# Decode step on one core: batch rows eight times each, one output transfer that closes the program, and another last part of wd

## The chip, the cores and the metric

One core of a Trainium2 chip. The metric is the device time of one execution in microseconds (us). Beside it the profile gives a *span*, from the first to the last recorded instruction; the time is always larger, by 1.6 to 2.0 us here. (The record does not say where the time begins; below, all of the difference is put at the end of the span.) Engines: PE (matmul; PEld is its weight load), DVE (vector), ACT (scalar), POOL (GpSimd), SP (sync, which issues most transfers).

## The reference

Batch 4, one query token, model width D = 640, 32 heads of 192, 4096 cached positions, MLP width F = 1536, all bf16:

```python
x  = A_x                                            # (4, 1, 640)
h  = x + attention(layernorm(x), k_cache, v_cache, wq) @ wo
h2 = h + (silu(ln(h) @ w_gate) * (ln(h) @ w_up)) @ w_down   # ln = layernorm
return h2                                           # (4, 1, 640)
```

The two caches are (4, 32, 4096, 192), 201 MB each. Nearly all of the 424 MB that the kernel reads is cache.

## The kernel before

SP queues all bulk loads in order: wq, then the K and V tiles of 32 units (6.3 MB each), then wo, w_gate, w_up and w_down (`wd`). A unit is multiplied on DVE, summed on PE, exponentiated on ACT and multiplied with V on PE. The parts that the change touches are the dense layers around that loop. Each of those spreads over four 32-column groups of the PE: group n computes the n-th quarter of the output columns for the 4 batch rows, and puts them at partitions 32n to 32n+3.

```python
for lo, hi in ((0, 6), (6, 10), (10, CF)):          # wd in three transfers; CF = 12
    ...dma("sp", wdsb[:, lo:hi, :] <- wd rows lo:hi)
...
kot = op("dve", tensor_copy(OT[:, :, :] <- psT[:, 0:B * JW]))     # 192 elements per partition
for j in range(JW): womm(j)                         # 4 matmuls each, lhsT=OT[:, :, j]: 4 columns
zg = op("dve", memset(PB[0][:, 0:FQ], 0.0)); zg = op("dve", memset(PB[1][:, 0:FQ], 0.0))
ln2 = layer_norm(psH[:, 0:DQ], [wo_done])
...                                                 # gate and up: lhsT=lnT[:, c, 0:B]
for c in range(CF):
    for n in range(4):
        a = op("pe", matmul(psH[32 * n:32 * n + B, 0:DQ], lhsT=guT[:, c, 0:B],
                            rhs=wdsb[:, c, n * DQ:(n + 1) * DQ], ...), [gut, wd_land[c], ln2])
a = op("dve", tensor_copy(out=outsb[:, 0:DQ], in_=psH[:, 0:DQ]), [a])
fin = [dma("sp" if n < 2 else "act", out[:, 0, n * DQ:(n + 1) * DQ] <-
           outsb[32 * n:32 * n + B, 0:DQ], S_out, [a]) for n in range(4)]
with nc.Block() as block:
    pr.emit(block, [fin[-1]])                       # SP waits for all four; then the end barrier
```

## Time and profile before

| | before |
|---|---|
| time, median of the first 3 runs | 990.11 us (989.95 to 990.49) |
| span of the profiled run, its time | 988.26 us, 989.84 us |
| DMA | 429 GB/s mean over the span |
| busy: PE, DVE, ACT | 59%, 56%, 12% |

From the profile page of the kernel before: the mean busy share of the 16 DMA engines in 40 equal slices of the span (9 is 90% or more), and the packets of ACT's queue, q10.

```profile
DMA  9999999999999999999999999999999999999997
...
q10 hardware_dynamic: 48, 0.01, 0.0%
```

The transfers never stop until the last slice. So what gets faster *inside* that stream should be hidden by it. The chain that ended last shows where the stream lets go (start, us, what):

```profile
946.95 38.09 DMA wd_sb<-in_B_w_down_dram
985.03 0.04 issue
985.08 0.46 PE pb L571 x8
985.54 0.03 issue
985.57 0.32 DVE gu L574
```

What follows the wd load is exposed: eight matmuls, the DVE copy, the output and the end of the program. The timeline of the kernel before (start, us, engine, line, operation; in brackets the idle time before, and what ended it):

```profile
960.47 0.36 DVE L551 CAST OT<-pb 128x192 bf16<-128x192 f32 x1 [1.25 <-PE pb L497]
...
966.67 5.92 PE L504 MATMUL pb<-wo_sb,OT 128*4 128x160 bf16 x192 [6.23 <-DMA wo_sb<-in_A_wo_dram]
...
984.32 1.19 PE L571 MATMUL pb<-wd_sb,guT 128*4 128x160 bf16 x24 [0.48 <-DMA wd_sb<-in_B_w_down_dram]
985.08 0.10 PEld L571 LDWEIGHTS pb<-wd_sb,guT 128*4 128x4 bf16 x8 [0.39 <-DMA wd_sb<-in_B_w_down_dram]
985.57 0.32 DVE L574 CAST gu<-pb 128x160 bf16<-128x160 f32 x1 [2.76 <-PE pb L571]
985.92 0.67 SPq L575 DMA_DIRECT2D out_dram<-gu  x2
985.92 0.81 ACTq L575 DMA_DIRECT2D out_dram<-gu  x2
```

wd rows 6 to 9 are taken up at 984.32, rows 10 and 11 at 985.08: the PE waits for each. The wo and OT lines start long before, and wait for data. The end of the program in the view of its closing line (engine, operation, minimum/median/maximum in ns, first and last start); the branch is the first instruction after SP's wait for the output:

```profile
L578 POOLq DRAIN  x1: 611/611/611, 4.9 to 4.9; - x1
...
L578 SPq COMPARE_BRANCH  x1: 33/33/33, 987.7 to 987.7; - x1
...
L578 PEldq EVENT_SEMAPHORE  x1: 51/51/51, 988.0 to 988.0; - x1
...
L578 SPq EVENT_SEMAPHORE  x1: 17/17/17, 988.2 to 988.2; - x1
```

SP passes the last barrier about 0.2 us after the other engines.

### The profile page before, as it was taken

How to read it: one execution, taken by the hardware profiler on the slowest of the kernel's cores; microseconds unless marked ns; L12 is line 12 of the kernel's file. 1: busy time of each engine (PE TensorE's matmuls, PEld its weight loads, DVE VectorE, ACT ScalarE, POOL GpSimd, SP SyncE). 2: the span in 40 equal slices, each digit the busy share in tenths (PEclk: the TensorE clock that was granted, in tenths of full speed). 3: DMA queues.
4: the chain of work that ended last, by engine and by line, in shares of the span. 5: the costliest groups of instructions: out<-in, count | busy, mean ns of one | idle time of the engine just before them, and what ended most of it. 6: DMA issues, size and time to landing. Idle time of an engine off the chain costs nothing.

```text
span 988.3 us, 9469 instructions
## 1 busy us (share of the span) xinstructions
PE 579.3 (59%) x4409; PEld 129.0 (13%) x2941; DVE 553.3 (56%) x454; ACT 117.1 (12%) x376; POOL 3.7 (0%) x18
## 2 busy tenths in 40 slices
PE   1677555666555576556566655656665555765554
PEld 0011011110101111001111110111101011110023
DVE  2486555566645556655556665555666455566621
ACT  0311111110111110011111011111101111100120
POOL 1000000000000000000000000000000000000000
PEclk9898777887777888777788777788877778887775
DMA  9999999999999999999999999999999999999997
GB/s 401 428 440 426 434 436 426 440 434 430 436 426 440 434 432 436 426 438 434 432 436 426 438 434 432 436 426 438 434 432 436 426 438 434 432 436 426 438 433 327
DMA packets 10583, 424.39 MB, mean 429 GB/s; under 512 B 1232, under 2 KB 1232, under 8 KB 1744
## 3 DMA queue, kind: packets, MB, share of 16 engines
q1 hardware_dynamic: 10528, 424.29, 99.5%
q8 instruction: 5, 0.08, 0.0%
q10 hardware_dynamic: 48, 0.01, 0.0%
q14 instruction: 2, 0.02, 0.0%
HBM read 424.29 MB, written 0.01 MB: 429 GB/s over the span
## 4 chain that ended last, share of the span: by engine, by line
DMA 67%; PE 18%; DVE 12%; issue 1%; SPq 1%; DVEq 0%
DMA k<-in_A_k_cache_dram 63%; DVE prod L412 12%; PE pb L161 11%; PE pb L462 4%; DMA wd_sb<-in_B_w_down_dram 4%; PE pb L420 2%; SPq L365 0%; DVE sc L425 0%; PE pb L468 0%; DVEq L412 0%; SPq L391 0%; SPq L385 0%; PE pb L571 0%; SPq L330 0%; PE pb L434 0%
## 5 line engine op out<-in xcount | busy, mean ns | idle before, releaser
L412 DVE TENSOR_TENSOR prod<-k,qball 128x6144 f16<-128x6144 bf16 x128 | 426.3, 3351 | 220.9 <-DMA k<-in_A_k_cache_dram 220.9
L161 PE MATMUL pb<-prod,identH 128*128 128x512 f16 x1408 | 384.3, 429 | 0.0
L420 PE MATMUL pb<-prod,identH 128*128 128x512 f16 x128 | 58.1, 454 | 339.9 <-DVE prod L412 339.9
L425 DVE TENSOR_REDUCE sc<-pb 128x32 f32<-128x512 f32 x128 | 88.0, 688 | 107.2 <-PE pb L161 107.2
L477 ACT ACTIVATE otmp<-pb,minv 128x192 f32<-128x192 f32 x32 | 13.4, 420 | 650.8 <-PE pb L462 650.8
L420 PEld LDWEIGHTS pb<-prod,identH 128*128 128x128 f16 x128 | 13.2, 103 | 586.1 <-DVE prod L412 481.2
L462 PE MATMUL pb<-v,pbuf 128*8 128x384 bf16 x1984 | 86.0, 326 | 0.0
L453 ACT ACTIVATE pbuf<-sc,negM 32x128 bf16<-32x128 f32 x128 | 73.4, 574 | 4.9
L462 PEld LDWEIGHTS pb<-v,pbuf 128*8 128x8 bf16 x1984 | 45.4, 87 | 28.8
L481 DVE SCALAR_TENSOR_TENSOR orow<-pb,minv,otmp 128x192 f32<-128x192 f32 x32 | 13.4, 418 | 55.1 <-ACT otmp L477 55.1
L497 PEld LDWEIGHTS pb<-orow,here 128*128 128x128 f32 x256 | 33.5, 192 | 73.7 <-issue 71.1
L497 PE MATMUL pb<-orow,here 128*128 128x48 f32 x256 | 31.7, 267 | 1.1 <-DVE orow L481 1.1
L453 ACT ACTIVATION_READ_ACCUMULATOR pbuf<-sc,negM 32x1 f32 x128 | 31.7, 248 | 0.0
L447 ACT ACTIVATE negM<-pb 128x4 f32<-128x4 f32 x32 | 5.5, 173 | 161.0 <-PE pb L443 161.0
L468 PEld LDWEIGHTS pb<-lsb,headm 128*128 128x128 f32 x64 | 12.3, 194 | 74.8 <-issue 71.2
L443 PE MATMUL pb<-negMc,ones_row 1*128 1x4 f32 x64 | 12.2, 258 | 11.9 <-DVE negMc L438 11.9
L434 PE MATMUL pb<-identF,msb 128*1 128x128 f32 x64 | 12.1, 270 | 9.8 <-DVE msb L430 9.8
L438 DVE TENSOR_REDUCE negMc<-pb 1x4 f32<-1x128 f32 x32 | 8.9, 279 | 15.1 <-PE pb L434 15.1
L443 PEld LDWEIGHTS pb<-negMc,ones_row 1*128 1x128 f32 x64 | 9.4, 183 | 21.3 <-DVE negMc L438 21.3
L468 PE MATMUL pb<-lsb,headm 128*128 128x1 f32 x64 | 9.2, 213 | 2.7 <-ACT pbuf L453 2.7
L490 ACT ACTIVATE here<-place 128x131 f32 (+1 forms) x32 | 10.0, 312 | 0.9
L430 DVE TENSOR_REDUCE msb<-sc 128x1 f32<-128x128 f32 x32 | 9.1, 286 | 1.1
(68 smaller groups left out, 84.8 us busy)
## 6 DMA issues: line engine op xcount, KB each, us to landing
k<-in_A_k_cache_dram SPq DMA_DIRECT2D x32, 6144.0 KB, 39.5
v<-in_A_v_cache_dram SPq DMA_DIRECT2D x31, 6144.0 KB, 25.5
wq_sb<-in_A_wq_dram SPq DMA_DIRECT2D x1, 7680.0 KB, 21.5
k<-in_A_v_cache_dram SPq DMA_DIRECT2D x1, 6144.0 KB, 39.2
wo_sb<-in_A_wo_dram SPq DMA_DIRECT2D x1, 5760.0 KB, 25.0
wo_sb<-in_A_wo_dram SPq DMA_DIRECT2D x1, 1920.0 KB, 26.9
wg_sb<-in_B_w_gate_dram SPq DMA_DIRECT2D x1, 1920.0 KB, 31.2
wu_sb<-in_B_w_up_dram SPq DMA_DIRECT2D x1, 1152.0 KB, 33.5
```

Of the source, the lines that this page charges most:

```text
L161: return e.add_instruction(mybir.InstMatmult(name=e.bass.get_next_instruction_name(), engine=mybir.EngineType.PE, start_tensor_calc=start, ...
L412: op("dve", lambda e: e.tensor_tensor(out=prod[BUF[k]][:, :, :], in0=kslot[u % 2][:, k * QT:(k + 1) * QT, :], in1=qball[:, bass.ds(u + pr. ...
L420: op("pe", lambda e, j=j: (e.matmul if j == 0 else partial(held_matmul, e))(psR[k][:, 0:QT * R], lhsT=identH[:, :], rhs=prod[BUF[k]][:, :, ...
L425: op("dve", lambda e: e.tensor_reduce(sc[u % 2][:, k * QT:(k + 1) * QT], psR[k][:, 0:QT * R].rearrange("q (t r) -> q t r", r=R), AX.X, ALU ...
L434: op("pe", lambda e: e.matmul(psS[0:1, XT], lhsT=msb[:, 0:1], rhs=identF[:, :], start=True, stop=True), [g("rmax", u), g("negM", u - 1), p ...
L443: op("pe", lambda e: e.matmul(psS[:, XB], lhsT=ones_row[0:1, :], rhs=negMc[0:1, :], start=True, stop=True), [g("hmax", u), g("negM", u - 1 ...
L453: op("act", lambda e, h=h, r=r: e.activation(out=pbuf[r, :, h], in_=sc[u % 2][r, :], func=ACTF.Exp, bias=negM[r, h:h + 1], scale=alpha, ac ...
L462: op("pe", lambda e, t=t, n=n: e.matmul(psO[32 * n:32 * n + 8, 0:2 * DH], lhsT=pbuf[:, t:t + 2, :].rearrange("q t m -> q (t m)"), rhs=vsrc ...
L468: op("pe", lambda e: e.matmul(psS[:, XL], lhsT=headm[:, :, :].rearrange("q r m -> q (r m)"), rhs=lsb[:, :], start=True, stop=True), [g("ex ...
L477: op("act", lambda e: e.activation(out=otmp[:, :], in_=psO[:, 0:DH], func=ACTF.Copy, scale=minv[:, 0:1]), [g("pv", u), g("minv", u), g("st ...
L481: op("dve", lambda e: e.scalar_tensor_tensor(out=orow[:, :], in0=psO[:, DH:2 * DH], scalar=minv[:, 1:2], in1=otmp[:, :], op0=ALU.mult, op1 ...
L497: op("pe", lambda e, i=i: e.matmul(psT[:, bass.ds(JW * at_unit(u)[0], JW)], lhsT=here[:, NI - 1 - i:NI - 1 - i + 128], rhs=orow[:, JW * i: ...
```

## The change

The 32 partitions of a column group now hold each batch row eight times (partition 32n + 8b + r, r = 0 to 7) instead of 4 rows and 28 unused ones. Weights then have 32 columns, the matmuls fill all 128 partitions of PSUM, and most of the clears of PSUM fall away. All 16 output rows lie 8 partitions apart, so that a single transfer can fetch them. ACT issues that transfer, waits for it and closes the program; the GpSimd drain at the end is left out. And wd lands as 6, 5 and 1 rows.

```diff
-    OT = sb("OT", [128, B, JW], BF16)
+    OT = nc.alloc_sbuf_tensor_at("OT", [128, JW, 32], BF16, offset=at(qball))
...
-    for k in (0, 1, 2, 3, 5, 7):
+    for k in (5, 7):
         zp = op("dve", lambda e, k=k: e.memset(PB[k][:, 0:2 * DH], 0.0))
...
-        out=spread[:, :].rearrange("q (n r) -> q n r", n=4)[:, :, 0:B],
-        in_=identF[0:4 * B, 0:4 * B].rearrange("q (b n) -> q n b", b=B)), [zp, c2])
+        out=spread[:, :].rearrange("q (n b r) -> q n b r", n=4, b=B),
+        in_=identF[...].rearrange("q (b n) -> q n b", b=B)[:, :, :, None].broadcast_to([4 * B, 4, B, RB])), [c2])
...
-    for lo, hi in ((0, 6), (6, 10), (10, CF)):
+    for lo, hi in ((0, 6), (6, 11), (11, CF)):
...
-                psH[32 * n:32 * n + B, 0:DQ], lhsT=OT[:, :, j], ...
+                psH[32 * n:32 * n + 32, 0:DQ], lhsT=OT[:, j, :], ...
...                                      # gate, up and wd matmuls likewise
-    zg = op("dve", lambda e: e.memset(PB[0][:, 0:FQ], 0.0), [...])
-    zg = op("dve", lambda e: e.memset(PB[1][:, 0:FQ], 0.0))
...
-    fin = [dma("sp" if n < 2 else "act", lambda e, n=n: e.dma_start(
-        out[:, 0, n * DQ:(n + 1) * DQ], outsb[32 * n:32 * n + B, 0:DQ]), S_out, [a]) for n in range(4)]
-    with nc.Block() as block:
-        pr.emit(block, [fin[-1]])
+    fin = dma("act", lambda e: e.dma_start(
+        out[:, 0, :].rearrange("b (n d) -> n b d", n=4),
+outsb[0:128:RB, 0:DQ]), S_out, [a])
+    with nc.Block(no_gpsimd_drain=True) as block:
+        pr.emit(block, "act", [fin])
```

More of the change, by code (lines that the diff above doesn't have):

```diff
@@ L78, in waits, with emit @@
         return out
-    def emit(self, block, final):
+    def emit(self, block, closer, final):
         for ops in self.ops.values():
@@ L146, in body @@
                     one(e, t)
-                if eng == "sp":
+                if eng == closer:
                     for d in final:
@@ L194, in build_kernel @@
     OFF = (H - 4) * NI + NI - 1
+    RB = 32 // B
     QS = 2.0 ** -4
@@ L286, in build_kernel @@
     pool_done = op("pool", lambda e: e.memset(pbuf[:, :, :], 0.0), [c4])
-    zp = op("dve", lambda e: e.memset(spread[:, :], 0.0))
-    for k in (0, 1, 2, 3, 5, 7):
+    for k in (5, 7):
         zp = op("dve", lambda e, k=k: e.memset(PB[k][:, 0:2 * DH], 0.0))
@@ L293, in build_kernel @@
     kspread = op("dve", lambda e: e.tensor_copy(
-        out=spread[:, :].rearrange("q (n r) -> q n r", n=4)[:, :, 0:B],
-        in_=identF[0:4 * B, 0:4 * B].rearrange("q (b n) -> q n b", b=B)), [zp, c2])
+        out=spread[:, :].rearrange("q (n b r) -> q n b r", n=4, b=B),
+        in_=identF[0:4 * B, 0:4 * B].rearrange("q (b n) -> q n b", b=B)[:, :, :, None].broadcast_to([4 * B, 4, B, RB])), [c2])
     ksel = op("dve", lambda e: e.tensor_copy(
         out=sel[:, :, :].rearrange("q b (h i) -> q b h i", h=4),
-        in_=identF[:, :].rearrange("q (h r) -> q r h", h=4)[:, 0:B, :, None].broadcast_to([128, B, 4, 32])))
+        in_=identF[:, :].rearrange("q (h r) -> q r h", h=4)[:, 0:32:RB, :, None].broadcast_to([128, B, 4, 32])))
     kquad = op("dve", lambda e: e.tensor_scalar(
@@ L338, in build_kernel @@
                 a = op("pe", lambda e, k=k, c=c, n=n, rhs=rhs, mm=mm: mm(
-                    e, PB[k][32 * n:32 * n + B, 0:2 * DH], lhsT=lnT[:, c, 0:B], rhs=rhs,
-                    start=(c == 0), stop=(c == CD - 1)), [ln1, wq_land, zp])
+                    e, PB[k][32 * n:32 * n + 32, 0:2 * DH], lhsT=lnT[:, c, :], rhs=rhs,
+                    start=(c == 0), stop=(c == CD - 1)), [ln1, wq_land])
             if c == CD - 1:
@@ L504, in womm @@
             a = op("pe", lambda e, n=n: e.matmul(
-                psH[32 * n:32 * n + B, 0:DQ], lhsT=OT[:, :, j], rhs=wosb[:, j, n * DQ:(n + 1) * DQ], start=False,
+                psH[32 * n:32 * n + 32, 0:DQ], lhsT=OT[:, j, :], rhs=wosb[:, j, n * DQ:(n + 1) * DQ], start=False,
                 stop=(j == JW - 1), skip_group_check=True), [kot, wo_land[j]])
@@ L550, in build_kernel @@
     o_t(u)
-    kot = op("dve", lambda e: e.tensor_copy(out=OT[:, :, :].rearrange("q b j -> q (b j)"), in_=psT[:, 0:B * JW]), [tk["oT", u]])
+    kot = op("dve", lambda e: e.tensor_copy(
+        out=OT[:, :, :].rearrange("q j (b r) -> q j b r", b=B),
+        in_=psT[:, 0:B * JW].rearrange("q (b j) -> q j b", b=B)[:, :, :, None].broadcast_to([128, JW, B, RB])),
+        [tk["oT", u], tk["tt", u, NQ - 1]])
     for j in range(JW):
         wo_done = womm(j)
-    zg = op("dve", lambda e: e.memset(PB[0][:, 0:FQ], 0.0), [g("red", u, NQ - 1), g("rsum", u, NQ - 1)])
-    zg = op("dve", lambda e: e.memset(PB[1][:, 0:FQ], 0.0))
     ln2 = layer_norm(psH[:, 0:DQ], [wo_done])
@@ L561, in build_kernel @@
                 a = op("pe", lambda e, k=k, w=w, c=c, n=n: e.matmul(
-                    PB[k][32 * n:32 * n + B, 0:FQ], lhsT=lnT[:, c, 0:B], rhs=w[:, c, n * FQ:(n + 1) * FQ],
-                    start=(c == 0), stop=(c == CD - 1)), [ln2, wu_land[c] if k else wg_land, zg])
+                    PB[k][32 * n:32 * n + 32, 0:FQ], lhsT=lnT[:, c, :], rhs=w[:, c, n * FQ:(n + 1) * FQ],
+                    start=(c == 0), stop=(c == CD - 1)), [ln2, wu_land[c] if k else wg_land, g("rsum", u, NQ - 1)])
         if k == 0:
@@ L571, in build_kernel @@
             a = op("pe", lambda e, c=c, n=n: e.matmul(
-                psH[32 * n:32 * n + B, 0:DQ], lhsT=guT[:, c, 0:B], rhs=wdsb[:, c, n * DQ:(n + 1) * DQ],
+                psH[32 * n:32 * n + 32, 0:DQ], lhsT=guT[:, c, :], rhs=wdsb[:, c, n * DQ:(n + 1) * DQ],
                 start=False, stop=(c == CF - 1), skip_group_check=True), [gut, wd_land[c], ln2])
     a = op("dve", lambda e: e.tensor_copy(out=outsb[:, 0:DQ], in_=psH[:, 0:DQ]), [a])
-    fin = [dma("sp" if n < 2 else "act", lambda e, n=n: e.dma_start(
-        out[:, 0, n * DQ:(n + 1) * DQ], outsb[32 * n:32 * n + B, 0:DQ]), S_out, [a]) for n in range(4)]
-    with nc.Block() as block:
-        pr.emit(block, [fin[-1]])
+    fin = dma("act", lambda e: e.dma_start(
[3 more added lines that the diff above has]
+        pr.emit(block, "act", [fin])
     eg.close()
```

## The prediction

> **What bounds the kernel now.** The DMA stream. The page's DMA row reads 9 in 39 of 40 slices, mean 429 GB/s, and DMA is 67% of the chain of waits; PE is busy 59%, DVE 56%, ACT 12%. The last 38.09 us link of the chain is the wd load, taken up by the PE at 985.08 us. Work before that point costs nothing unless it delays a transfer or reaches past it. So of 990.11 us this change can touch about the last 3.2 us of the 988.3 us span.
>
> **The tail now** (timeline from 984 us and the starts of its last instructions): wd rows 6-9 are taken up at 984.32, rows 10-11 at 985.08; matmuls end near 985.5; DVE copy 985.57 to 985.90; four output transfers, two each from SP and ACT, the last from ACT 986.47 to 986.73; SP's wait ends 987.67; closing barrier, to 988.26.
>
> **Removed.**
> 1. Three of four output issues. One ACT issue of 16 rows should take 0.42 us (as the x load, also 16 rows, took on ACT), ending near 986.35 instead of 986.73. Issue end to end of wait was 0.94 us; four times the rows may add 0.05. The Trainium skill, "DMA: Bandwidth & Descriptors", section "Issuing engines are not separate DMA queues", says that issuing from several engines only saves sequencer issue time; here each queue still issued two in a row. Gain 0.35 us, on the path.
> 2. SP as closer. After its wait SP took 0.14 us to its drain, and passed the final barrier at 988.24, 0.26 us after the other engines (987.98). With ACT this may go: gain 0 to 0.25, on the path.
> 3. The GpSimd drain: it sat at 4.9 us, off the path. Gain 0.
> 4. PSUM clears (2.42 us at the start, 0.76 at 960.9): hidden behind the wq wait to 22.4 and the wo wait to 966.6. Gain 0.
>
> **Added and moved.**
> 5. Weights of 32 columns instead of 4. The skill, "TensorE: Matmul & The Clock Gate", section "LDWEIGHTS (loading the stationary operand)", gives columns/1.2 ns: 27 ns, an estimate. The wo phase now paces 31 ns per matmul, so the load should stay hidden. Even 10% on the 5.92 us wo phase is absorbed: the first 24 wd matmuls end near 983.8, before the next rows land.
> 6. The OT copy writes 1536 elements, not 192: from 0.36 us to an estimated 1.7; done by 962.3, wo lands at 966.6. Hidden.
> 7. wd split 6/5/1 instead of 6/4/2. A row is 0.38 us of stream, (985.08-984.32)/2. Rows 6-10 come at about 984.70; their 20 matmuls, five groups of four at about 0.13 us, keep the PE until about 985.35, past the last row's landing at 985.08. The matmuls then end at about 985.65, not 985.5: a loss of 0.15 us, on the path.
>
> **Sum.** -0.35 - 0.15 (expected of 2) + 0.15 - small effects = -0.4 to -0.5 us: 989.65 us, range 989.0 to 990.3. Faster by over 2%: 0.01; within 2%: 0.98; slower: 0.01.
>
> **What would show it.** One output issue of about 0.42 us on ACT and the wait ending near 987.4; last wd matmuls queued behind the five groups, not waiting for DMA; wo phase still near 6 us; DMA stream ending at the same time; loop stretches identical.
>
> **What would make it wrong.** Wider weights slowing wo by 3 us or more, pushing the MLP past the wd landing; 16 output rows serialised on few DMA engines; a slow ACT drain; the wd split having the other sign.

## The result, and the profile after

| | before | after |
|---|---|---|
| time, median of 6 runs | 990.43 us (989.95 to 990.75) | 990.23 us (990.12 to 990.60) |
| ratio after/before | | 0.9999, 95% interval 0.9986 to 1.0012 |
| span, time of the profiled run | 988.26, 989.84 us | 988.37, 990.19 us |

The ratio is the mean time of one kernel's fast runs over that of the other's in the same rounds, so it is not quite the ratio of the medians. The kernel before alone, over all rounds, ran between 989.66 and 990.75 us. A step of some tenths of a us cannot be seen in the time, so the steps are read from the profile, where each one is a distance between two records.

From the profile page of the changed kernel:

```profile
DMA  9999999999999999999999999999999999999997
...
q10 hardware_dynamic: 52, 0.01, 0.0%
```

Its chain of waits at the end:

```profile
946.58 38.12 DMA wd_sb<-in_B_w_down_dram
984.70 0.04 issue
984.75 1.02 PE pb L573 x18
985.76 0.02 issue
985.79 0.33 DVE gu L576
```

The chain now leaves the DMA stream at 984.70, at the landing of rows 6 to 10, and spends 1.02 us on the PE instead of 0.46. The timeline says the same:

```profile
960.49 1.76 DVE L552 CAST OT<-pb 128x1536 bf16<-128x1536 f32 x1 [1.25 <-PE pb L498]
966.68 5.85 PEld L505 LDWEIGHTS pb<-wo_sb,OT 128*32 128x32 bf16 x192 [6.35 <-issue]
966.71 6.02 PE L505 MATMUL pb<-wo_sb,OT 128*32 128x160 bf16 x192 [6.26 <-DMA wo_sb<-in_A_wo_dram]
...
984.75 0.99 PE L573 MATMUL pb<-wd_sb,guT 128*32 128x160 bf16 x24 [0.83 <-DMA wd_sb<-in_B_w_down_dram]
985.79 0.33 DVE L576 CAST gu<-pb 128x160 bf16<-128x160 f32 x1 [2.91 <-PE pb L573]
986.14 1.13 ACTq L577 DMA_DIRECT2D out_dram<-gu  x1
```

All 24 remaining matmuls run in one piece from 984.75 on; the landing of row 11 no longer ends any wait. The single output issue takes 1.13 us, longer than two of the old ones in a row on ACT (0.81). And the close:

```profile
L581 ACTq COMPARE_BRANCH  x1: 38/38/38, 987.9 to 987.9; - x1
...
L581 SPq EVENT_SEMAPHORE  x2: 17/17/17, 947.7 to 988.3; - x2
L581 PEldq EVENT_SEMAPHORE  x2: 51/51/51, 985.9 to 988.3; - x2
```

SP no longer lags at the end. The whole tail, from records of single instructions and packets in the two traces ("stream end" is the end of the last wd data packet, "wait over" the start of the branch after the wait for the output), in us:

```
                                        before    after   after - before
stream end, from the span's start      984.582  984.609      +0.03
stream end -> closing DVE copy           0.984    1.177      +0.19
copy -> first output issue               0.350    0.358      +0.01
first output issue -> wait over          1.762    1.779      +0.02
wait over -> end of span                 0.586    0.451      -0.14
end of span -> end of time               1.58     1.82       +0.24
sum: time of the profiled run          989.84   990.19       +0.35
```

So in the profiled pair nothing was won: 0.19 us went to the wd split, the one transfer took as long as the four, and what the close seemed to win inside the span came back after it. The medians moved by -0.20 us; neither figure stands out of the scatter. One step can be seen in many runs, though: the time minus the span (spans are rounded to 0.1 us in the record) is 1.52 to 1.63 us in 27 runs of the kernel before, mean 1.57, and 1.75 to 1.82 in the six of the changed one, mean 1.79.

### The profile page after: what moved, and what is told of

Its sections match the earlier page's. It is cut to its first block, busy times and chain, and to the rows that moved or that the text cites. A ratio compares the mean times of both kernels' runs of the same rounds, so it can differ in the third digit from the quotient of the medians.

```text
span 988.4 us, 9461 instructions
## 1 busy us (share of the span) xinstructions
PE 580.1 (59%) x4409; PEld 129.6 (13%) x2941; DVE 552.5 (56%) x447; ACT 117.1 (12%) x376; POOL 3.6 (0%) x18
## 4 chain that ended last, share of the span: by engine, by line
DMA 67%; PE 18%; DVE 12%; issue 1%; SPq 1%; DVEq 0%
DMA k<-in_A_k_cache_dram 63%; DVE prod L413 12%; PE pb L161 12%; PE pb L463 4%; DMA wd_sb<-in_B_w_down_dram 4%; PE pb L421 2%; SPq L366 0%; DVE sc L426 0%; PE pb L469 0%; DVEq L413 0%; PE pb L573 0%; SPq L386 0%; SPq L392 0%; PE pb L435 0%; SPq L331 0%
```

## The experiments

Thirteen kernels ran, all built from the changed kernel. Runs with no rounds give one profile and one time (state unknown); their verdicts rest on distances inside the profile. They came on four chips, each with times of the kernel before beside them; the distances are compared with its one profile. `pool_third_642`: GpSimd's transfer has a semaphore of its own.

### The wd split alone: wd_642

```diff
-    for lo, hi in ((0, 6), (6, 11), (11, CF)):
+    for lo, hi in ((0, 6), (6, 10), (10, CF)):
```

> The changed kernel with wd landing as 6, 4 and 2 rows again. Theory A (the 6/5/1 split makes the PE the last to finish): rows 6-9 are taken up near 984.3 us, the last eight matmuls wait for the landing near 985.08, the closing DVE copy starts near 985.58 instead of 985.79, and the output issue stays at about 1.13 us, so the span falls by about 0.2 us, to 988.2. Rival B (the copy starts later because 32-column weights are slower): the copy still starts at 985.7 or later.

Its timeline:

```profile
984.54 1.22 PE L573 MATMUL pb<-wd_sb,guT 128*32 128x160 bf16 x24 [0.43 <-DMA wd_sb<-in_B_w_down_dram]
985.31 0.14 PEld L573 LDWEIGHTS pb<-wd_sb,guT 128*32 128x32 bf16 x8 [0.36 <-DMA wd_sb<-in_B_w_down_dram]
985.82 0.33 DVE L576 CAST gu<-pb 128x160 bf16<-128x160 f32 x1 [2.75 <-PE pb L573]
```

The copy did *not* start at 985.58 as expected, nor did the span fall: the whole stream ended 0.2 us later in this run (984.814). The absolute clock was the wrong thing to forecast. The distance is the right one: from stream end to copy 1.004 us here, against 1.177 with 6/5/1, and the PE waits for the last landing again. Theory A holds and B does not: with 32-column weights and the old split the distance is that of the kernel before (0.984). Over all runs it is 1.10 to 1.18 with 6/5/1 (eight profiles) and 0.98 to 1.00 with 6/4/2 (five).

### What makes the one transfer slow

Three runs, and two later ones, change only the pattern of the output.

```diff
 out_four:         four transfers, outsb[32 * n:32 * n + 32:RB, 0:DQ], from SP, SP, ACT, ACT
-        out[:, 0, :].rearrange("b (n d) -> n b d", n=4), outsb[0:128:RB, 0:DQ]
 out_flat_dst:
+        out[:, 0, :].rearrange("b (n d) -> (b n) d", n=4), outsb[0:128:RB, 0:DQ]
 out_packed_src:
+        out[:, 0, :].rearrange("b (n d) -> n b d", n=4), outsb[0:16, 0:DQ]
 out_packed_flat:
+        out[:, 0, :].rearrange("b (n d) -> (b n) d", n=4), outsb[0:16, 0:DQ]
 out_step2_flat:
+        out[:, 0, :].rearrange("b (n d) -> (b n) d", n=4), outsb[0:32:2, 0:DQ]
```

All but out_four give a wrong result.

> The changed kernel with four output transfers of 4 rows again, from rows 8 partitions apart; ACT still closes and there is still no GpSimd drain. Theory A (the one transfer of 16 rows costs the sequencer 1.13 us to issue, more than two small ones in a row): the ACT pair takes 0.75 to 0.9 us from first start to last end, and from DVE copy to the end of ACT's wait it is about 1.8 us. Rival C (rows 8 partitions apart make any issue slow): each of the four issues takes 0.6 us or more.

> Wrong result on purpose: the one transfer writes 16 rows in contiguous order (no 4x4 permutation in DRAM), source rows still 8 partitions apart. Theory D (the permuted destination, 4x4 rows against 16 source rows, costs the issue): the issue falls from 1.13 to about 0.42 to 0.55 us. Rival C (source stride of 8 partitions): it stays at about 1.1 us. Rival E (16 rows to store, or ACT's first issue for a long time): it stays as well.

> Wrong result on purpose: the one transfer reads 16 neighbouring partitions, destination still permuted 4x4. Theory D: the issue stays at about 1.1 us. Rival C (source stride): it falls to about 0.42 to 0.55 us. Rival E: it stays.

> Wrong result on purpose: the one transfer reads 16 neighbouring partitions and writes 16 neighbouring rows, so neither stride nor permutation is left. So far, stride with flat rows took 1.82 us from issue start to the end of ACT's wait, permutation with neighbouring partitions 1.88 us, both together 1.78 us. Theory F (either stride or permutation alone takes the transfer off a fast course; without both it is fast): issue 0.3 to 0.45 us, first packet about 0.75 us after the issue starts, wait over after about 1.2 us. Rival G (16 rows, or something else in the changed kernel, is slow whatever the pattern): first packet after 1.2 us or more, wait over after about 1.8 us.

> Wrong result on purpose: one transfer, flat rows in DRAM, source every second partition of 0 to 31. If any step other than 1 is slow: issue near 0.59 us, first packet 1.25 us after its start, wait over after 1.8 us, as with step 8. If only the wide spread over partitions is slow: 0.34, 0.85 and 1.42 us, as with neighbouring partitions.

The output issues in the timelines of out_four (two lines), out_flat_dst, out_packed_src and out_packed_flat, in this order:

```profile
986.16 1.39 SPq L577 DMA_DIRECT2D out_dram<-gu  x2
986.17 1.99 ACTq L577 DMA_DIRECT2D out_dram<-gu  x2
```

```profile
986.11 0.59 ACTq L577 DMA_DIRECT2D out_dram<-gu  x1
```

```profile
986.12 1.22 ACTq L577 DMA_DIRECT2D out_dram<-gu  x1
```

```profile
986.03 0.34 ACTq L577 DMA_DIRECT2D out_dram<-gu  x1
```

The single records, in us from the start of the (first) issue:

```
one transfer of 16 rows                issue   first data packet   wait over
after: step 8, permuted rows           1.129        1.289            1.779
out_packed_src: step 1, permuted       1.222        1.386            1.876
out_flat_dst: step 8, flat             0.592        1.249            1.817
out_step2_flat: step 2, flat           0.608        1.262            1.834
out_packed_flat: step 1, flat          0.337        0.846            1.418
four transfers of 4 rows, two queues
before: step 1                       0.26-0.52      0.757            1.762
out_four: step 8                     0.59-1.36      1.342            3.073
```

Two things follow. First, the length of the issue record is not the cost: out_flat_dst issued in half the time of the changed kernel, and its wait ended no earlier. What counts is the time from the start of the issue to the first packet, which is 0.76 to 0.85 us for a source of neighbouring partitions written to plain rows, and 1.25 to 1.39 us as soon as *either* the source steps over partitions *or* the destination is permuted (4x4 rows against 16). One cause is enough, and both together cost no more (1.289). That is Theory F; the rivals "16 rows" and "ACT's first issue for a long time" fall with out_packed_flat, which has both and is fast. I had expected C or D to be right alone; neither is. Theory A, that the number of rows makes the issue long, falls too: in out_four the four strided transfers of 4 rows took 3.07 us together. (The wait of out_packed_flat ended after 1.42 us, not after the expected 1.2.) Second, a step of 2 is as slow as one of 8. Why a step or a permutation costs half a microsecond before the first packet, no run here shows, nor whether it is the new order of the rows or their two nested steps.

The page of out_packed_flat, beside the 52 packets of the changed kernel:

```profile
q10 hardware_dynamic: 64, 0.01, 0.0%
```

In both, 32 of these belong to the x load and 16 are output rows. What is left are completion writes: 16 with flat rows, 4 with the permutation. So the permuted transfer used 4 DMA engines and the flat one 16, as the Trainium skill has it ("DMA: Bandwidth & Descriptors", section "Why a DMA increments its semaphore by 16 and not by 1": the largest number up to 16 that divides the slowest dimension of both sides). But that is not what decides here: out_flat_dst used 16 engines too and was slow, and the data packets of the changed kernel all started within 0.11 us.

### The close

```diff
 sp_single:   dma("sp", ...) and pr.emit(block, "sp", [fin]); one transfer as in the change
 with_drain:
-    with nc.Block(no_gpsimd_drain=True) as block:
+    with nc.Block() as block:
```

> The changed kernel with the single transfer issued and waited for by SP, which closes. If the long issue belongs to the transfer's pattern: 1.1 us on SP too, and wait over 1.8 us after the issue starts. If it belongs to ACT: 0.4 us. The close after SP's wait: 0.59 us as in the kernel before, against 0.45 with ACT, so the span grows by 0.1 to 0.15 us if SP as closer costs what it seemed to.

> The changed kernel with the GpSimd drain at the end put back. If that drain costs nothing (it ran early, at 4.9 us, in the kernel before), the close after ACT's wait stays at 0.45 us and the span moves only by what the stream's end moves. If it is what shortened the close, the close goes back to about 0.59 us.

The slow pattern is as slow on SP (first packet after 1.30 us, wait over after 1.79), although SP's issue record is only 0.70 us long:

```profile
986.15 0.70 SPq L577 DMA_DIRECT2D out_dram<-gu  x1
```

So the slow start does not belong to ACT. From the closing line of sp_single:

```profile
L581 PEldq EVENT_SEMAPHORE  x2: 51/51/51, 985.9 to 988.3; - x2
L581 SPq EVENT_SEMAPHORE  x2: 17/17/17, 988.1 to 988.6; - x2
```

SP starts its last pass about 0.26 us after the others again, and ends it 0.23 us after them; by that the span grows. But the time does not: it was 990.16 us, as with ACT.

```
                     closer, drain  wait over -> others' pass  -> span end  span end -> time  wait over -> time
before               SP, yes               0.36                  0.59            1.58              2.16
sp_single            SP, no                0.43                  0.66            1.56              2.22
after                ACT, no               0.45                  0.45            1.82              2.27
with_drain           ACT, yes              0.40                  0.40            1.98              2.38
```

("Others' pass" is the end of the last barrier on the engines that did not lag.) In the first three rows the time ends 1.79 to 1.82 us after the others' pass, whether SP lags or not; in the other profiles, with_drain apart, it is 1.78 to 1.82. The lag lies inside the span but not on the way to the end of the time. Without the lag the change's close is about 0.1 us *longer* than before; why, no run shows. Leaving out the drain put 0.05 us more into the close and 0.16 us less after the span, neither of the two outcomes expected. These are single profiles, and the 1.98 us did not come back in the five runs of four_adjacent_6411_sp below, which have the drain too (time minus span 1.75 to 1.84).

### Correct versions without the slow pattern

Replicating the rows in the other order, 32n + 4r + b, puts the four batch rows side by side, so that four fast transfers are possible again while 32-column weights stay.

```diff
-        out=spread[:, :].rearrange("q (n b r) -> q n b r", n=4, b=B),
+        out=spread[:, :].rearrange("q (n r b) -> q n r b", n=4, b=B),
...                              # sel and OT likewise
 four_adjacent_642:  four transfers of outsb[32 * n:32 * n + B, 0:DQ], SP SP ACT ACT; wd 6/4/2
 two_adjacent_642:   two, SP and ACT, of outsb[32 * n + 28:32 * n + 36, 0:DQ], n = 0 and 2; wd 6/4/2
 pool_third_642:     four transfers from SP, ACT, SP, GpSimd; wd 6/4/2
 four_adjacent_6411: as four_adjacent_642, wd ((0, 6), (6, 10), (10, 11), (11, CF))
 four_adjacent_6411_sp: the same, closed by SP, with the drain
```

> Right result: batch rows replicated in the other order (partition 32n + 4r + b), so four transfers of 4 neighbouring partitions each are possible again; wd in 6, 4 and 2 rows; ACT still closes, no GpSimd drain, 32-column weights stay. Theory F (stride of 8 partitions slows the issue): SP's and ACT's second issues take 0.26 to 0.30 us again against 0.59 in the run with four strided transfers, first packets 0.75 us after each issue starts, from first issue to end of wait 1.76 us, tail from last wd packet to span end about 3.55 us against 3.68 of the kernel before and 3.77 of the changed one; time about 0.1 us under the kernel before, inside its noise. Rival G (another part of the change slows the output): the second issues still take about 0.59 us.

> Right result: rows in the order 32n + 4r + b, wd 6/4/2, and two transfers, one from SP and one from ACT, each of 8 neighbouring partitions that straddle two column groups (28 to 35 and 92 to 99), destination permuted 2x4. Theory F (a permuted destination is slow whatever the number of rows): each issue takes 0.7 us or more and first packets come 1.2 us or more after the issue starts, so it ends no earlier than the changed kernel. If the permutation costs by the row: about 0.6 to 0.7 us, and the wait ends near 1.5 us after the issue.

> Right result: four transfers of neighbouring partitions over three issuing engines (SP two, ACT one, GpSimd one), wd 6/4/2. SP's second issue ends near 0.67 us after the first starts, and lands 1.2 us after its own start, near 1.6 us. If GpSimd's transfer lands by then, the wait ends at 1.55 to 1.6 us after the first issue instead of 1.77, and the tail is about 0.15 us shorter; if its descriptors are slow, the wait ends at 2 us or later.

> Right result: four transfers of neighbouring partitions, wd in 6, 4, 1 and 1 rows, so that after the last landing one group of four matmuls is left and the PE is idle before it. From last wd packet to the closing DVE copy: 0.98 to 1.00 us with 6/4/2, 1.11 to 1.18 with 6/5/1; here about 0.90. Tail from last packet to span end about 3.45 us. In the time of the whole kernel this is too small to see.

> Right result: four transfers of neighbouring partitions, wd 6/4/1/1, closed by SP with the GpSimd drain, as the kernel before closes. If SP's late pass of the barrier is only moved out of the span when ACT closes: span end 0.59 us after the wait (0.44 with ACT), time minus span 1.58 us (1.82 with ACT), so from the end of the wait to the end of the time 2.16 us against 2.26 with ACT; tail from last wd packet to the end of the time 5.17 us, against 5.26 in the kernel before and 5.58 in the changed one. If SP's late pass is a real cost in the time: time minus span stays at 1.8 us and the whole is 0.15 us longer than with ACT. In the median, under 0.1 us less than the kernel before, which the rounds will not resolve.

```
                        stream end  first issue    wait over    tail in   median (runs)   kernel before,
                         -> copy    -> wait over   -> time      the span                  same rounds
four_adjacent_642         0.994       1.769          2.25        3.559    990.31 (5)      989.97 (9)
two_adjacent_642          0.999       2.093          2.24        3.896    990.56 (5)      989.97 (9)
pool_third_642            0.991       2.048          2.22        3.835    990.85 (5)      990.14 (9)
four_adjacent_6411        0.899       1.754          2.26        3.447    990.20 (5)      990.14 (9)
four_adjacent_6411_sp     0.866       1.747          2.53        3.695    990.34 (5)      990.31 (9)
before                    0.984       1.762          2.16        3.682
after                     1.177       1.779          2.27        3.765
```

- four_adjacent_642: the second issues take 0.28 and 0.26 us again, and each engine's pair is as short as before (0.67 and 0.82 us, against 0.67 and 0.81), so nothing else in the change slows the output. Theory F holds.

```profile
985.89 0.67 SPq L577 DMA_DIRECT2D out_dram<-gu  x2
985.89 0.82 ACTq L577 DMA_DIRECT2D out_dram<-gu  x2
```

- two_adjacent_642: 8 neighbouring partitions with a 2x4 permutation are slow as well (first packet after 1.38 us); the cost is not by the row.
- pool_third_642: GpSimd's issue took 0.65 us and its first packet came 0.35 us after that of SP's second transfer; the wait ended later, not earlier.
- four_adjacent_6411: with one row in each of the last two parts the PE is idle before the last landing, and the copy comes 0.90 us after the stream's end, as expected:

```profile
984.45 1.09 PE L573 MATMUL pb<-wd_sb,guT 128*32 128x160 bf16 x24 [0.48 <-DMA wd_sb<-in_B_w_down_dram]
985.22 0.11 PEld L573 LDWEIGHTS pb<-wd_sb,guT 128*32 128x32 bf16 x4 [0.23 <-DMA wd_sb<-in_B_w_down_dram]
985.60 0.32 DVE L576 CAST gu<-pb 128x160 bf16<-128x160 f32 x1 [2.68 <-PE pb L573]
```

- four_adjacent_6411_sp was to keep that and get the shorter close back. It did not: SP this time did not lag at the barrier, but stood for about 0.4 us between the branch after its wait and its drain (0.14 us in the kernel before), so the close took 0.73 us, and the end of the time came 2.53 us after the wait. Of the two outcomes, the second came nearer: the time minus the span was 1.80 us (1.8 expected), and the whole was 0.27 us longer than with ACT (0.15 expected). It fits the rule above: a pause *before* the last barrier holds up the others, and the time still ended 1.80 us after their pass; only a lag of SP alone *after* it costs no time. The place of SP's pause differs between these programs; what it waits for there stays open.

None of these is shown to be faster than the kernel before: every ratio's 95% interval, such as 0.9987 to 1.0014 for four_adjacent_6411, holds 1. The best of them has the shortest tail of a correct kernel inside the span (3.447 us), but to the end of the time its tail is 5.27 us against 5.26 before (sums of the distances for the one profiled run each).

## Why the prediction was right or wrong

The forecast of about 0.4 to 0.5 us gained was wrong; the measured medians lie 0.20 us apart inside a scatter of about 1 us, the profiled pair even 0.35 us the other way. The range and "within 2%" held, which says little, since both were wider than the change. (The terms of the sum that are written out give -0.35; the rest, "small effects", was not explained.)

- **What bounds the kernel: right.** The DMA stream ended within 0.03 us of where it did in the profiled pair, and only what comes after counted.
- **Step 1, "Gain 0.35 us, on the path": this step failed.** The forecast was 0.42 + 0.94 + 0.05 = 1.41 us from issue to the end of the wait; it took 1.78, with an issue of 1.13 instead of 0.42. The size was right for a transfer that the change does not make. I took the issue of the x load (0.42 us) as the model for the output, because both have 16 rows. The x load has neighbouring partitions and plain rows; the output steps over 8 partitions and permutes 4x4. With the x load's pattern the wait ends 1.418 us after the issue starts (out_packed_flat), which is 0.34 us less than the 1.762 before, about the gain that was predicted. That close a hit is partly luck: the issue took 0.34 us there, not 0.42, and the rest 1.08, not 0.99. With the real pattern it is 1.779: gain -0.02. "16 output rows serialised on few DMA engines", which the prediction named as a danger, is not the cause: it used 4 engines, but its packets started within 0.11 us, only after 1.29.
- **Step 2, "gain 0 to 0.25, on the path": failed too.** In the span the close did become 0.135 us shorter, near the 0.15 assumed. But I read SP's lag at the last barrier as part of the path because it sat at the end of the span. The time ended 1.78 to 1.82 us after the other engines' pass in 14 of the 15 profiles; measured to the end of the time, the close lost 0.1 us (2.16 to 2.27).
- **Step 3, the drain, "Gain 0": not settled at that size.** It lies at 4.9 us and is not waited for, but taking it out also changed the barrier: wait over to time 2.27 us without, 2.38 with, one profile each.
- **Step 4, PSUM clears, "Gain 0": right.** wq and wo still ended the waits of the PE.
- **Step 5, wider weights: right.** The wo phase took 6.02 us against 5.92. The profile's groups by shape give the mean weight load of that phase as 119 ns with 4 columns and 140 with 32, of the wd phase as 104 and 136. The Trainium skill's columns/1.2 ns ("TensorE: Matmul & The Clock Gate", section "LDWEIGHTS (loading the stationary operand)"), for 28 columns more, is 23 ns (an estimate). The trace agrees roughly with this difference, 21 and 32 ns, but not with the predicted 27 ns for one load: the records are about five times as long. The matmuls' pace hides them.
- **Step 6, the OT copy: right.** 1.76 us where 1.7 was estimated, hidden before the wo landing.
- **Step 7, the wd split, "a loss of 0.15 us": right in sign and mechanism.** 0.19 us in the pair, 0.10 to 0.20 over the runs, and undone with 6/4/2.

So the sum lost both of its gains and kept its loss.

## What to carry to other kernels

With 4 to 16 rows, the time before a transfer's first packet went with its pattern (0.76 to 0.85 us plain, 1.25 to 1.39 us stepped or permuted) and not with the number of rows: predict a new transfer only from one with the same step over partitions and the same nesting of rows on both sides, and expect that merging several plain transfers into one irregular one can win nothing (1.76 against 1.78 us here). When a stream of transfers ends the kernel, cut its last parts by how long the engine behind them needs per row, not as small as possible at the very end only: a fat part just before the last moves the wait to the engine (from stream end to copy 1.10 to 1.18 us with 6/5/1, 0.98 to 1.00 with 6/4/2, 0.87 to 0.90 with 6/4/1/1). And before counting the end of a span as a gain, check that the reported time moves with it.

## What the Trainium skill lacked or had wrong

- "DMA: Bandwidth & Descriptors" has, for this chip, no word on what a step over partitions or a permuted destination costs a small transfer from SP or ACT. Here either took the first packet from 0.76 to 0.85 us after the issue's start to 1.25 to 1.39 us, and the end of the wait for 16 rows from 1.42 to 1.78 to 1.88 us.
- The same page, section "Rules for kernel authors", advises to coalesce many small transfers into one. The runs show that this holds where the merged pattern stays plain (1.42 us, in a run with a wrong result, against 1.76 us for four), and not where it does not (1.78 us).
- The same page, section "Issuing engines are not separate DMA queues", says that several issuing engines only save issue time. A third one, GpSimd, did not save even that here: its issue took 0.65 us against 0.26 us for ACT's second, which it replaced, and the wait 2.05 us against 1.77 us.
- No page says how the device time used here relates to the end of the last recorded instruction (the nearest, "Runtime: NRT & Kernel Launch", is about two other figures). Here the time was 1.56 to 1.98 us longer than the span, and a lag of SP at the last barrier lengthened the span by 0.23 us and not the time.
